# A conditional general path without SyncE and VectorE, the default order of its blocks, and two modulation loads merged into one

## The chip, the cores and the metric

One core of one Trainium2 chip runs the whole computation in one launch. The metric is the device time of that core in microseconds; the lower, the better. The engines are PE (matmuls; PEld is its weight load), DVE and ACT (vector and scalar work), POOL (GpSimd), and SP, which here only issues DMAs. Each engine has a sequencer that reads its own list of instructions in order; work between engines is ordered by semaphores. Sixteen DMA engines move the data.

## The reference

A transformer block on 2048 tokens of width 512: an adaptive layer norm, a linear attention of 32 heads with 16 columns each, and a gated feed-forward of width 1376. Cut to what matters:

```python
mod = (silu(c) @ w_mod).reshape(1, 6, 1, -1)
sa, ca, ga, sb, cb, gb = (mod[:, i] for i in range(6))
h = layernorm(x) * (1 + ca) + sa
q, k, v = split(h @ wqkv)                       # 32 heads of 16
phi(t) = concat(softmax(t @ w_phi), softmax(-(t @ w_phi)))
o = phi(q) @ (phi(k)^T v) / (phi(q) . sum_s phi(k) + 1e-6)
x = x + ga * (o @ wo)
h = layernorm(x) * (1 + cb) + sb
x = x + gb * ((sigmoid(h @ w_gate) * (h @ w_up)) @ w_down)
```

The kernel's main path takes the softmaxes' exponentials without subtracting the maximum first. That is safe while the logits are small. So the kernel works out a bound on them and writes a flag, 0 or 1. With 1, a second, general path computes everything again with the maximum subtracted and overwrites the output. With the inputs that are timed here the flag is 0 and the general path is not run.

## The kernel before, in words

**Tiling.** The tokens are 16 tiles of 128. The first part normalises each tile, transposes it into `h1T`, and builds K, V and their product over all tiles. The second takes the tiles in chunks of 1, 1, 2, 4, 4 and 4: attention output, output projection, second norm, feed-forward. A tile's result is summed by DVE from PE's `y_ps` and the residual (task `fin`, L905) and stored by SP (task `st`, L907). The last chunk's sums run in the order 12, 13, the first half of 15, 14, and then the second half of 15, which is the last store, of 64 KB.

**Order.** A planner written into the kernel (`Graph.order`) lists every piece of work as a task with an assumed cost, a due time and a release time, and simulates five engines and one DMA queue; the order that comes out is the order in which the instructions are written to each engine's list. Tables of hand-set shifts (`DUE`, `REL`, `ENG`) move single tasks. Loads are tasks on SP; a load's release time is the earliest moment in the planner's clock. The planner lets a load of a number of bytes end at a fixed rate after the one before it.

**Modulation weights.** `w_mod` has six column groups of 512. Two loads bring groups 0 and 1 early. Three more follow on SP at L965: `ga` (group 2), `m2` (groups 3 and 4), `gb` (group 5). After them comes `wo` (L966), then four transposing DMAs into `h1T` (L1111), then the feed-forward weights. Groups 3 and 4 are read by `modc2` (L1015), group 5 by `gb` (L1198), both about 58 us into the run.

**Semaphores of DMAs.** The framework gives DMAs eight semaphores in turn, each DMA the next one, and a DMA on a semaphore waits until the DMA that used it before has landed. A DMA that runs on all 16 DMA engines raises its semaphore once for each. SP issues 71 DMAs in the main path (18 loads, 36 transposes and 17 stores) and ACT issues 2.

**The conditional.** Before the sum of tile 12 the flag is read into a register of each engine that will need it (`load_flag`, L913; the loads are the `TENSOR_LOAD` at L914). After the whole main path comes

```python
    with tc.If(fv_box[0] > 0, preferred_fallthrough_block=False):   # L1306
        emit(order2)
```

`order2` is a second plan, `G2`, which holds the general path: `features` (L1241) for the softmaxes, and the same `downstream` as the main path, with its transposing DMAs and stores on SP and its vector work on DVE. All five engines take part, so each of them has a compare-and-branch at L1306. Where the flag is 0, an engine passes through an arm in which it raises semaphores by what the skipped body would have added, so that the waits that follow hold for either arm. `preferred_fallthrough_block=False` puts that arm directly behind the compare, and the body behind the arm.

**The end.** After the conditional (these instructions carry L1333) SP waits for every semaphore still in use, and then all engines pass through an exchange of semaphores and a drain, by which the kernel ends.

Of the kernel before, what the change touches and what calls it, by code (L numbers as in the profile page):

```python
# [21 lines left out]
F_LAST = F - (FT - 1) * P  # L22
NG = 8
VC = DH + 1
# [402 lines left out]
def kernel(  # L427
# [56 lines left out]
    VS = 4  # L484
# [41 lines left out]
    def bank(name, shape=None, dtype=FP32):  # L526
        return Buf("bank", shape or [P, 512], dtype, name)

    def small(name, shape):
        return Buf(name if name in CAPS else "ks", shape, FP32, name)  # L530

    def emit(order):
        for t in order:
            for b in t.bufs:
                if b.cls not in ("h2", "hm", "vaug"):
                    get(b)
            t.fn(t.eng)
# [4 lines left out]
    def kv_tasks(G, acc, t, ph, va, due, parts=((0, 8),), chain=()):  # L542
        for a, b in parts:
            def kv(e, a=a, b=b):
                for g in range(a, b):
                    pe.matmul(acc[g // 4][:, (g % 4) * HC:(g % 4 + 1) * HC], lhsT=ph[:, g * P:(g + 1) * P],  # L546
                              rhs=vaug[va.slot][:, 4 * g:4 * g + 4, :].rearrange("p h d -> p (h d)"),
                              start=(t == 0 and g % 4 == 0), stop=(t == NT - 1), skip_group_check=True)
            halves = [("kvacc", h) for h in range(2) if a < 4 * h + 4 and b > 4 * h]
            G.add(f"kv{t}.{a}", {"PE": 0.031 * (b - a)}, kv, r=[("phi", t, a), ("vaug", t)], w=[*halves, *chain],  # L550
                  bufs=[ph, va] + [acc[h] for _, h in halves], due=due)
# [359 lines left out]
    fv_box = []  # L911

    def load_flag():  # L913
        fv_box.append(nc.values_load(flag[0:1, 0:1], min_val=0, max_val=1,  # L914
                                     skip_runtime_bounds_check_because="written as 0 or 1"))

    def bound_tasks(G, due):
        for j in range(KT):
# [42 lines left out]
    load_x("x2", 8, 12, LX[0])  # L961
    load_x("x3", 12, 16, LX[1])
    load("wq", ["wq"], lambda e: sp.dma_start(wqk_sb[:, :, 0:D], wqkv_v[:, :, 0:D]), 512 * K1, LD[0], rel=LD[0])
    for nm, c0, c1, due in (("ga", 2, 3, LD[1]), ("m2", 3, 5, LD[2]), ("gb", 5, 6, LD[3])):
        load("wm" + nm, ["wmod_" + nm], lambda e, c0=c0, c1=c1: sp.dma_start(wmod_sb[:, :, c0 * D:c1 * D], wmod_v[:, :, c0 * D:c1 * D]), (c1 - c0) * 512 * K1, due, rel=due)  # L965
    load("wo", ["wo_raw"], lambda e: sp.dma_start(wo_sb[:], A_wo.rearrange("(j p) n -> p j n", p=P)), 512 * K1, LD[4], rel=LD[4])  # L966
    load("wg", ["wg"], lambda e: sp.dma_start(wg_sb[:], B_w_gate.rearrange("(j p) n -> p j n", p=P)), 1376 * K1, LD[5], rel=LD[5])
# [171 lines left out]
    for t in range(NT):  # L1139
# [8 lines left out]
        def f_v(e, t=t, vp=vp):  # L1148
            for j in range(KT):
                pe.matmul(vp[:], lhsT=h1T[:, j, t * P:(t + 1) * P], rhs=wv_sb[:, j, :], start=(j == 0), stop=(j == KT - 1))  # L1150
# [44 lines left out]
    def f_mm(e, ps, c0):  # L1195
        for j in range(KT):
            pe.matmul(ps[:], lhsT=scb[:, j, :], rhs=wmod_sb[:, j, c0:c0 + D], start=(j == 0), stop=(j == KT - 1))
    G.add("gb", {"PE": 0.87}, lambda e: f_mm(e, gb_ps, 5 * D), r=["scb", "wmod_gb"], w=["gb"], bufs=[gb_ps], due=MISC[2])  # L1198
    G.add("gbc", {"ACT": 0.6}, lambda e: act.mul(gb_bc[:], gb_ps[:], 0.5), r=["gb", "modc2ps"], w=["gbc"], bufs=[gb_ps], due=MISC[2] + 1.0)
    ga_sb = Buf("r2k", [P, D], FP32, "ga_sb")  # L1200
    G.add("ga", {"PE": 0.87}, lambda e: f_mm(e, ga_ps, 2 * D), r=["scb", "wmod_ga"], w=["ga"], bufs=[ga_ps], due=MISC[2])
# [34 lines left out]
    order = G.order()  # L1236
    emit(order)

    G2 = Graph(CAPS)

    def features(t, side, key):  # L1241
        sv = "p (h s j) -> p s h j" if side else "p (s h j) -> p s h j"

        pk = bank("pk_g")

        def f1(e):
            for j in range(KT):
                pe.matmul(pk[:], lhsT=h1T[:, j, t * P:(t + 1) * P], rhs=wqk_f[:, j, side * D:(side + 1) * D], start=(j == 0), stop=(j == KT - 1))
        G2.add(f"gp{side}{t}", {"PE": 0.9}, f1, w=[("gp", side, t), "chain"], bufs=[pk])
        ext = small("ext", [P, 2, H])  # L1250
        dd = [Buf("r2k", [P, H, DH], FP32, "dd") for _ in range(2)]
        ph = Buf("r2k", [P, 2 * H * DH], BF16, "gphi")

        def f2(e):
            pv = pk[:].rearrange("p (h j) -> p h j", j=DH)
            dve.tensor_reduce(ext[:, 0], pv, axis=AX.X, op=ALU.max)
            dve.tensor_reduce(ext[:, 1], pv, axis=AX.X, op=ALU.min)
            for s in range(2):
                dve.tensor_tensor(dd[s][:], pv, ext[:, s].unsqueeze(2).to_broadcast([P, H, DH]), op=ALU.subtract)

        def f3(e):
            for s in range(2):
                act.activation(dd[s][:], dd[s][:], ACT.Exp, scale=1.0 - 2.0 * s)

        def f4(e):
            for s in range(2):
                dve.tensor_reduce(ext[:, s], dd[s][:], axis=AX.X, op=ALU.add)
            dve.reciprocal(ext[:], ext[:])
            for s in range(2):
                dve.tensor_tensor(ph[:].rearrange(sv, s=2, j=DH)[:, s], dd[s][:],  # L1270
                                  ext[:, s].unsqueeze(2).to_broadcast([P, H, DH]), op=ALU.mult)
        G2.add(f"gd{side}{t}", {"DVE": 2.8}, f2, r=[("gp", side, t)], w=[("gd", side, t), "chain"], bufs=[pk, ext] + dd + [ph])
        G2.add(f"ge{side}{t}", {"ACT": 1.2}, f3, r=[("gd", side, t)], w=[("ge", side, t), "chain"], bufs=dd)
        G2.add(f"gn{side}{t}", {"DVE": 2.8}, f4, r=[("ge", side, t)], w=[key, "chain"], bufs=[ext] + dd + [ph])
        return ph

    acc = [bank(f"gacc{i}") for i in range(2)]
    for t in range(NT):
        ph = features(t, 1, ("phi", t, 0))
        vp = bank("gv")  # L1280
        va = Buf("vaug", None, None, "gva")

        def f_v(e, t=t, vp=vp):
            for j in range(KT):
                pe.matmul(vp[:], lhsT=h1T[:, j, t * P:(t + 1) * P], rhs=wv_sb[:, j, :], start=(j == 0), stop=(j == KT - 1))
        G2.add(f"gV{t}", {"PE": 0.9}, f_v, w=[("v", t), "chain"], bufs=[vp], due=t)
        G2.add(f"gva{t}", {"ACT": 0.6}, lambda e, vp=vp, va=va: act.copy(vaug[va.slot][:, :, 0:DH], vp[:].rearrange("p (h d) -> p h d", d=DH)),
               r=[("v", t)], w=[("vaug", t), "chain"], bufs=[vp, va], due=t)
        kv_tasks(G2, acc, t, ph, va, t, chain=["chain"])
    kvbd_tasks(G2, acc)  # L1290
    eT2 = [Buf("eT", [P, NG, 512], BF16, f"geT{cq}") for cq in range(4)]
    for cq in range(4):
        for tl in range(4):
            t = 4 * cq + tl
            ph = features(t, 0, ("gphq", t))
            tp = bank("gtp", [P, NG, P], BF16)

            def f_t(e, ph=ph, tp=tp):
                for g in range(NG):
                    pe.transpose(tp[:, g, :], ph[:, g * P:(g + 1) * P], ident[:])  # L1300
            G2.add(f"gT{t}", {"PE": 0.5}, f_t, r=[("gphq", t)], w=[("gT", t), "chain"], bufs=[ph, tp], due=100.0 + t)
            G2.add(f"gTc{t}", {"ACT": 1.0}, lambda e, cq=cq, tl=tl, tp=tp: act.copy(eT2[cq][:, :, tl * P:(tl + 1) * P], tp[:]),
                   r=[("gT", t)], w=[("eT", cq, tl)], bufs=[tp, eT2[cq]], due=100.0 + t)
    downstream(G2, eT2, 200.0, False)
    order2 = G2.order()
    with tc.If(fv_box[0] > 0, preferred_fallthrough_block=False):  # L1306
        emit(order2)


# [28 lines left out]
```

## Time and profile before

| | us |
|---|---|
| runs | 216.2, 216.68, 217.49; median 216.68 |
| span of the profiled execution | 215.3 |
| PE busy | 202.7 (94%) |
| DVE busy | 166.1 (77%) |
| ACT busy | 113.0 (53%) |
| POOL busy | 101.3 (47%) |

The span runs from the first to the last instruction of the profiled execution; the time of a run also holds what lies around it. Register, branch, semaphore and DMA-issuing instructions are not counted as busy. By stretch, on PE:

| stretch, us | PE busy, us | granted clock |
|---|---|---|
| 0 to 60 | 55.86 | 1.00 |
| 60 to 90 | 29.24 | 1.00 |
| 90 to 145 | 53.62 | 1.00 |
| 145 to 198 | 52.74 | 1.00 |
| 198 to 216 | 11.20 | 0.88 |

Instruction code is itself brought in by DMA: the profile lists two queues of the kind "instruction", q8 with 14 packets of 16 KB and q14 with 15 packets, most of 8 KB. Each such packet runs on one of the sixteen DMA engines.

### The profile page before, as it was taken

How to read it: one execution, taken by the hardware profiler on the slowest of the kernel's cores; microseconds unless marked ns; L12 is line 12 of the kernel's file. 1: busy time of each engine (PE TensorE's matmuls, PEld its weight loads, DVE VectorE, ACT ScalarE, POOL GpSimd, SP SyncE). 2: the span in 40 equal slices, each digit the busy share in tenths (PEclk: the TensorE clock that was granted, in tenths of full speed). 3: DMA queues.
4: the chain of work that ended last, by engine and by line, in shares of the span. 5: the costliest groups of instructions: out<-in, count | busy, mean ns of one | idle time of the engine just before them, and what ended most of it. 6: DMA issues, size and time to landing. Idle time of an engine off the chain costs nothing.

```text
span 215.3 us, 4319 instructions
## 1 busy us (share of the span) xinstructions
PE 202.7 (94%) x1512; PEld 113.4 (53%) x1539; DVE 166.1 (77%) x447; ACT 113.0 (53%) x278; POOL 101.3 (47%) x133
## 2 busy tenths in 40 slices
PE   7998998999999999989999999999999999999980
PEld 2744454555666577857964544454444444444450
DVE  3799999988689999859989978999899871237340
ACT  3699987998959894345442233643211651235000
POOL 3859999999969999511552222403205210000000
PEclk9999999999999999999999999999999999999996
DMA  6997997970000210250614110233201231000111
GB/s 183 371 255 167 372 193 164 411 246 0 0 3 0 52 26 5 59 90 1 99 24 72 27 28 7 68 73 74 52 14 37 52 73 50 0 0 0 55 50 34
DMA packets 31423, 18.76 MB, mean 87 GB/s; under 512 B 20673, under 2 KB 29346, under 8 KB 31394
## 3 DMA queue, kind: packets, MB, share of 16 engines
q1 hardware_dynamic: 30864, 18.39, 33.2%
q8 instruction: 14, 0.23, 0.4%
q14 instruction: 15, 0.12, 0.2%
q10 hardware_dynamic: 530, 0.02, 0.1%
HBM read 11.58 MB, written 2.10 MB: 64 GB/s over the span
## 4 chain that ended last, share of the span: by engine, by line
PE 70%; DVE 9%; DMA 8%; SPq 4%; issue 2%; ACT 2%; POOL 1%; DVEq 0%; POOLq 0%
PE y_ps L895 16%; PE u_ps L854 15%; PE g_ps L854 15%; PE a_ps L762 5%; PE v_ps L1150 4%; DMA wqk_sb<-in_A_wqkv_dram 4%; PE k_ps L1146 3%; PE q_ps L1224 3%; SPq L1044 3%; DVE u L735 2%; DMA oT<-o 2%; DMA x_sb<-in_A_x_dram 2%; PE num L645 2%; PE kvacc L546 2%; PE g_ps L856 1%
## 5 line engine op out<-in xcount | busy, mean ns | idle before, releaser
L864 ACT ACTIVATE tg<-g_ps 128x512 bf16<-128x512 f32 (+4 forms) x66 | 28.9, 453 | 57.7 <-PE g_ps L854 43.8
L875 DVE SCALAR_TENSOR_TENSOR wmod_sb<-tg,u_ps 128x512 bf16<-128x512 bf16 (+4 forms) x63 | 29.7, 494 | 17.3 <-PE u_ps L854 9.4
L895 PE MATMUL y_ps<-wd_sb,wmod_sb 128*128 128x512 bf16 (+3 forms) x178 | 41.3, 366 | 0.4
L753 POOL TENSOR_TENSOR o<-u 128x512 bf16<-128x512 f32 x14 | 17.7, 1268 | 32.0 <-DVE u L720 15.0
L1168 POOL TENSOR_TENSOR phi<-e,ks 128x1024 bf16<-128x1024 bf16 (+2 forms) x22 | 31.4, 1454 | 0.5 <-DVE ks L1178 0.3
L854 PEld LDWEIGHTS <-wg_sb 128*128 128x128 bf16 (+1 forms) x252 | 21.6, 99 | 16.2 <-issue 1.0
L854 PEld LDWEIGHTS <-wu_sb 128*128 128x128 bf16 (+1 forms) x252 | 21.8, 99 | 15.2
L895 PEld LDWEIGHTS <-wmod_sb 128*128 128x128 bf16 (+1 forms) x187 | 17.9, 98 | 16.4
L854 PE MATMUL u_ps<-wT_sb,wu_sb 128*128 128x512 bf16 (+2 forms) x123 | 23.3, 322 | 0.2
L854 PE MATMUL g_ps<-wT_sb,wg_sb 128*128 128x512 bf16 (+2 forms) x121 | 23.2, 321 | 0.1
L854 PE MATMUL g_ps<-wqk_sb,wg_sb 128*128 128x128 bf16 (+4 forms) x127 | 19.8, 287 | 0.5 <-DVE wqk_sb L828 0.4
L1165 DVE TENSOR_REDUCE ks<-e 128x64 f32<-128x1024 bf16 (+2 forms) x22 | 19.7, 906 | 0.6 <-ACT e L1162 0.6
L854 PE MATMUL u_ps<-wqk_sb,wu_sb 128*128 128x128 bf16 (+4 forms) x127 | 19.6, 287 | 0.1
L905 DVE TENSOR_TENSOR ot<-y_ps,x 128x512 bf16<-128x512 f32 (+1 forms) x17 | 11.2, 656 | 9.8 <-PE y_ps L895 9.8
L1162 ACT ACTIVATE e<-k_ps 128x512 bf16<-128x512 f32 (+2 forms) x44 | 18.3, 499 | 0.3 <-POOL phi L1168 0.3
L762 PE MATMUL a_ps<-wo_sb,oT 128*128 128x512 bf16 x62 | 16.3, 379 | 1.2 <-DMA oT<-o 1.0
L1229 ACT ACTIVATE eT<-q_ps 128x512 bf16<-128x512 f32 x32 | 16.8, 618 | 0.9 <-PE q_ps L1224 0.9
L1146 PE MATMUL k_ps<-wqk_f,h1T 128*128 128x512 bf16 x60 | 15.9, 379 | 1.1 <-ACT h1T L1126 0.8
L1150 PE MATMUL v_ps<-wv_sb,h1T 128*128 128x512 bf16 x63 | 15.8, 379 | 0.1
L1224 PE MATMUL q_ps<-h1T,wqk_f 128*128 128x512 bf16 x60 | 15.1, 378 | 0.1
L1075 DVE BATCH_NORM_STATS2 st<-x_sb 128x6 f32<-128x512 bf16 x16 | 10.8, 676 | 3.3 <-DMA x_sb<-in_A_x_dram 3.3
L767 DVE TENSOR_TENSOR x<-a_ps,x_sb 128x512 f32<-128x512 f32 x16 | 10.9, 684 | 2.5 <-PE a_ps L762 2.3
(154 smaller groups left out, 322.3 us busy)
## 6 DMA issues: line engine op xcount, KB each, us to landing
wmod_sb<-in_w_mod_dram SPq DMA_DIRECT2D x4, 512.0 KB, 6.5
out_dram<-ot SPq DMA_DIRECT2D x15, 128.0 KB, 1.7
x_sb<-in_A_x_dram SPq DMA_DIRECT2D x3, 512.0 KB, 7.5
wg_sb<-in_B_w_gate_dram SPq DMA_DIRECT2D x1, 1376.0 KB
wu_sb<-in_B_w_up_dram SPq DMA_DIRECT2D x1, 1376.0 KB, 9.4
wd_sb<-in_B_w_down_dram SPq DMA_DIRECT2D x1, 1280.0 KB, 12.2
wqk_sb<-in_A_wqkv_dram SPq DMA_DIRECT2D x2, 512.0 KB, 4.3
wmod_sb<-in_w_mod_dram SPq DMA_DIRECT2D x1, 1024.0 KB, 8.3
```

The lines of the kernel that those rows point to most:

```text
L753: G.add(f"o{t}", {"POOL": 1.3, "DVE": 0.62}, lambda e, ub=ub, o=o: engine(e).tensor_tensor(o[:], ub[0][:].rearrange("p h d -> p (h d)"), u ...
L762: pe.matmul(ap_[:], lhsT=oT[:, j, :], rhs=wo_sb[:, j, :], start=(j == 0), stop=(j == KT - 1))
L854: pe.matmul(ps[:fsz, 0:n], lhsT=w[:, j, ft * P:ft * P + fsz], rhs=h[:, j, 0:n], start=(j == 0), stop=(j == KT - 1))
L864: G.add(f"tg{k}.{ft}", {"ACT": 0.13 + n * 0.00083}, lambda e, tg=tg, g_ps=g_ps, fsz=fsz, n=n: act.activation(tg[:fsz, 0:n], g_ps[:fsz, 0:n ...
L875: dve.scalar_tensor_tensor(hm_all[:fsz, hm[k].slot, ft, 0:n], tg[:fsz, 0:n], 1.0, u_ps[:fsz, 0:n], op0=ALU.add, op1=ALU.mult)
L895: pe.matmul(y[:, 0:c1 - c0], lhsT=hm_all[:fsz, hm[k].slot, ft, tl * P:(tl + 1) * P], rhs=wd_sb[:fsz, ft, c0:c1], start=(ft == 0), stop=(ft ...
L1146: pe.matmul(kp[:], lhsT=h1T[:, j, t * P:(t + 1) * P], rhs=wqk_f[:, j, D:2 * D], start=(j == 0), stop=(j == KT - 1))
L1150: pe.matmul(vp[:], lhsT=h1T[:, j, t * P:(t + 1) * P], rhs=wv_sb[:, j, :], start=(j == 0), stop=(j == KT - 1))
L1162: act.activation(ee[:, ha:hb, s, :], kp[:, ha * DH:hb * DH].rearrange("p (h j) -> p h j", j=DH), ACT.Exp, scale=1.0 - 2.0 * s)
L1165: dve.tensor_reduce(ks[:, ha:hb].rearrange("p h s -> p (h s)"), ee[:, ha:hb].rearrange("p h s j -> p (h s) j"), axis=AX.X, op=ALU.add)
L1168: pool.tensor_tensor(ph[:, ha * 32:hb * 32].rearrange("p (h j) -> p h j", j=DH), ee[:, ha:hb].rearrange("p h s j -> p (h s) j"), ks[:, ha: ...
L1224: pe.matmul(qp[:], lhsT=wqk_f[:, j, blk * P:(blk + 1) * P], rhs=h1T[:, j, cq * 512:(cq + 1) * 512], start=(j == 0), stop=(j == KT - 1))
```

## The change

Four things. The flag is read on PE, ACT and POOL only. The loads `m2` and `gb` become one load of groups 3 to 5 (1536 KB), and the task `gb` reads from it; the main path then has 72 DMAs. The general path is no longer planned: it is written out tile by tile, with PE, ACT and POOL alone. Maxima and sums that DVE took with one reduction become chains of halvings on POOL, reciprocals become two POOL instructions, transposes go through PE and ACT, and one POOL DMA stores the whole output. And the conditional is opened without `preferred_fallthrough_block`.

```diff
     def load_flag():
-        fv_box.append(nc.values_load(flag[0:1, 0:1], min_val=0, max_val=1,
-                                     skip_runtime_bounds_check_because="written as 0 or 1"))
+        fv_box.append(nc.values_load(flag[0:1, 0:1], engines=[mybir.EngineType.PE, mybir.EngineType.Activation, mybir.EngineType.Pool],
+                                     min_val=0, max_val=1, skip_runtime_bounds_check_because="written as 0 or 1"))
...
-    for nm, c0, c1, due in (("ga", 2, 3, LD[1]), ("m2", 3, 5, LD[2]), ("gb", 5, 6, LD[3])):
+    for nm, c0, c1, due in (("ga", 2, 3, LD[1]), ("m2", 3, 6, LD[2])):
         load("wm" + nm, ["wmod_" + nm], lambda e, c0=c0, c1=c1: sp.dma_start(wmod_sb[:, :, c0 * D:c1 * D], wmod_v[:, :, c0 * D:c1 * D]), (c1 - c0) * 512 * K1, due, rel=due)
...
-    G.add("gb", {"PE": 0.87}, lambda e: f_mm(e, gb_ps, 5 * D), r=["scb", "wmod_gb"], w=["gb"], bufs=[gb_ps], due=MISC[2])
+    G.add("gb", {"PE": 0.87}, lambda e: f_mm(e, gb_ps, 5 * D), r=["scb", "wmod_m2"], w=["gb"], bufs=[gb_ps], due=MISC[2])
...
-    G2 = Graph(CAPS)
...
-    downstream(G2, eT2, 200.0, False)
-    order2 = G2.order()
-    with tc.If(fv_box[0] > 0, preferred_fallthrough_block=False):
-        emit(order2)
+    def gen_fold(src, n, op, name):
...
+        while n > 1:
+            n //= 2
+            a, b = src[:, :, 0:n], src[:, :, n:2 * n]
+            if op == ALU.add:
+                pool.tensor_tensor(t[:, :, 0:n], a, b, op=ALU.add)
...
+    def gen_features(t, side):
...
+            m = gen_fold(ps[:], DH, ALU.min if s else ALU.max, "g_ex")
+            pool.tensor_tensor(dd[:], ps[:], m.unsqueeze(2).to_broadcast([P, H, DH]), op=ALU.subtract)
+            act.activation(dd[:], dd[:], ACT.Exp, scale=1.0 - 2.0 * s)
+            gen_recip(ext[:], gen_fold(dd[:], DH, ALU.add, "g_sum"), [P, H])
+            pool.tensor_tensor(ph[:, s], dd[:], ext[:].unsqueeze(2).to_broadcast([P, H, DH]), op=ALU.mult)
...
+    with tc.If(fv_box[0] > 0):
+        gen_keys()
+        for t in range(NT):
+            gen_tokens(t)
+        pool.dma_start(o_v[:, :, :], x_sb[:])
```

More of the change, by code (lines that the diff above doesn't have):

```diff
@@ L1237 @@
     emit(order)
-    G2 = Graph(CAPS)
[L1241 to L1283, printed above, removed]
+    def gen_tile(tag, shape, dtype, name):
+        return cst.tile(shape, dtype, name=name, tag=tag, bufs=1)
+    def gen_bank(i, shape=None, dtype=FP32):
+        return psp.tile(shape or [P, 512], dtype, name=f"g_bank{i}", tag=f"bank{i}", bufs=1)
+    def gen_fold(src, n, op, name):
+        r = src.shape[1]
+        t, d = gen_tile("r2k5", [P, r, n // 2], FP32, name), None
+        if op != ALU.add:
+            d = gen_tile("r2k4", [P, r, n // 2], FP32, name + "d")
+        while n > 1:
[3 more added lines that the diff above has]
+                pool.tensor_tensor(t[:, :, 0:n], a, b, op=ALU.add)
+            else:
+                a, c = (b, a) if op == ALU.min else (a, b)
+                pool.tensor_tensor(d[:, :, 0:n], a, c, op=ALU.subtract)
+                pool.tensor_scalar(d[:, :, 0:n], d[:, :, 0:n], 0.0, None, op0=ALU.max)
+                pool.tensor_tensor(t[:, :, 0:n], b, d[:, :, 0:n], op=ALU.subtract if op == ALU.min else ALU.add)
+            src = t
+        return t[:, :, 0]
@@ new lines, in gen_recip @@
+    def gen_recip(dst, src, shape):
+        half = mhalf[:, 0:1]
+        for _ in shape[1:-1]:
+            half = half.unsqueeze(1)
+        pool.tensor_tensor(dst, src, half.to_broadcast(shape), op=ALU.pow)
+        pool.tensor_tensor(dst, dst, dst, op=ALU.mult)
+    def gen_features(t, side):
+        pk = gen_bank(0)
+        for j in range(KT):
+            pe.matmul(pk[:], lhsT=h1T[:, j, t * P:(t + 1) * P], rhs=wqk_f[:, j, side * D:(side + 1) * D], start=(j == 0), stop=(j == KT - 1))
+        ps = gen_tile("x10", [P, H, DH], FP32, "g_pk")
+        act.copy(ps[:].rearrange("p h d -> p (h d)"), pk[:])
+        ph = gen_tile("r2k0", [P, 2, H, DH], BF16, "g_phi")
+        for s in range(2):
+            dd = gen_tile(f"x1{1 + s}", [P, H, DH], FP32, "g_dd")
+            ext = gen_tile(f"ks{s}", [P, H], FP32, "g_ext")
+            m = gen_fold(ps[:], DH, ALU.min if s else ALU.max, "g_ex")
[3 more added lines that the diff above has]
+            pool.tensor_tensor(ph[:, s], dd[:], ext[:].unsqueeze(2).to_broadcast([P, H, DH]), op=ALU.mult)
+        return ph[:].rearrange("p s h d -> p (s h d)")
@@ L1284, in f_v, with gen_keys @@
+    def gen_keys():
+        acc = [gen_bank(1 + i) for i in range(3)]
+        for t in range(NT):
+            ph = gen_features(t, 1)
+            vp = gen_bank(4)
             for j in range(KT):
                 pe.matmul(vp[:], lhsT=h1T[:, j, t * P:(t + 1) * P], rhs=wv_sb[:, j, :], start=(j == 0), stop=(j == KT - 1))
-        G2.add(f"gV{t}", {"PE": 0.9}, f_v, w=[("v", t), "chain"], bufs=[vp], due=t)
-        G2.add(f"gva{t}", {"ACT": 0.6}, lambda e, vp=vp, va=va: act.copy(vaug[va.slot][:, :, 0:DH], vp[:].rearrange("p (h d) -> p h d", d=DH)),
-               r=[("v", t)], w=[("vaug", t), "chain"], bufs=[vp, va], due=t)
@@ L1289 @@
[L1289 to L1303, printed above, removed]
@@ L1304 @@
-    downstream(G2, eT2, 200.0, False)
-    order2 = G2.order()
-    with tc.If(fv_box[0] > 0, preferred_fallthrough_block=False):
-        emit(order2)
+            va = vaug[t % VS]
+            act.copy(va[:, :, 0:DH], vp[:].rearrange("p (h d) -> p h d", d=DH))
+            for g in range(NG):
+                pe.matmul(acc[g // 3][:, (g % 3) * 136:(g % 3 + 1) * 136], lhsT=ph[:, g * P:(g + 1) * P],
+                          rhs=va[:, 8 * (g % 4):8 * (g % 4) + 8, :].rearrange("p h d -> p (h d)"),
+                          start=(t == 0 and g % 3 == 0), stop=(t == NT - 1), skip_group_check=True)
@@ new lines, in gen_keys @@
+        for g in range(NG):
+            kv = gen_tile("x10", [P, 8, VC], FP32, "g_kv")
+            act.copy(kv[:].rearrange("p h c -> p (h c)"), acc[g // 3][:, (g % 3) * 136:(g % 3 + 1) * 136])
+            pool.tensor_tensor(kvbd[:, g, 0:P].rearrange("p (h d) -> p h d", d=DH), kv[:, :, 0:DH], bm, op=ALU.mult)
+            z = gen_tile("ks0", [P, 8], FP32, "g_z")
+            pool.tensor_scalar(z[:], kv[:, :, DH], 0.5e-6, None, op0=ALU.add)
+            pool.tensor_tensor(kvbd[:, g, P:P + 8], z[:], bm[:, :, 0], op=ALU.mult)
@@ L1311 @@
+    with tc.If(fv_box[0] > 0):
+        gen_keys()
+        for t in range(NT):
+            gen_tokens(t)
+        pool.dma_start(o_v[:, :, :], x_sb[:])
 _INS = ['A_x', 'A_wqkv', 'A_w_phi', 'A_wo', 'B_x', 'B_w_gate', 'B_w_up', 'B_w_down', 'c', 'w_mod']
```

67 lines of the change are left out of this document (added).

## The prediction

> **What bounds the kernel now.** I read the shares first: PE is busy 94% of the span, its clock is full until the last slice, and the chain of waits is 70% PE. Nothing in the diff touches a PE instruction of the main path, so the time can only move where PE is *not* the bound: at the load it merges, and after PE's last matmul. So I went to the end. The last pieces of the chain of waits (start us, length us, what), then the timeline from 209.2 us on:
>
> ```profile
> 203.87 5.40 PE y_ps L895 x35
> 209.27 0.02 issue
> 209.29 0.42 DVE ot L905
> ```
> ```profile
> 209.29 0.42 DVE L905 TENSOR_TENSOR ot<-y_ps,x 128x256 bf16<-128x256 f32 x1 [0.51 <-PE y_ps L895]
> 209.74 0.33 SPq L907 DMA_DIRECT2D out_dram<-ot  x1
> ```
>
> The last useful act is the issue of the last store at 209.74; the span ends at 215.3 (the last semaphore event at 215.26). So 5.5 us are tail. What fills them are sequencer instructions, which the page does not count as busy; they show when the line of the conditional (L1306) and the line of the kernel's end (L1333) are asked for. Columns: count, duration ns min/median/max, first and last start in us.
>
> ```profile
> L1306 SPq EVENT_SEMAPHORE  x8: 17/17/17, 212.8 to 213.3; - x8
> L1306 SPq COMPARE_BRANCH  x2: 43/48/53, 210.1 to 213.4; - x2
> L1306 PEldq COMPARE_BRANCH  x2: 95/1890/3686, 206.4 to 209.4; - x2
> L1306 ACTq COMPARE_BRANCH  x2: 38/44/49, 198.7 to 199.0; - x2
> L1306 POOLq COMPARE_BRANCH  x2: 38/42/45, 177.2 to 177.4; - x2
> ...
> L1333 SPq EVENT_SEMAPHORE  x10: 17/28/28, 213.9 to 215.2; - x10
> L1333 SPq DRAIN  x3: 7/7/13, 214.4 to 214.8; - x3
> ```
>
> Each engine meets two branches: a compare that falls through into the "flag is 0" arm, where semaphores are raised by what the skipped body would have added, and a jump over the body. SP, which issues all 17 stores, raises eight DMA semaphores there, and the first it asks for is that of the last store, so all eight stand behind its landing. On PE the jump alone takes 3.686 us.
>
> **The tail as a sum.** Times to the hundredth are the trace's instruction records. Landing L = 212.81. Eight raises, 212.83 to 213.41: 0.58. Jump until SP's next instruction at 213.92: 0.51. Eight final waits to 214.44: 0.52, or 0.065 each. Drains and the exchange between the five engines, to 215.26: 0.82. From L to the end: 2.45.
>
> And L itself is late. The first line below are landings (min/median/max) of the three stores issued between 205.2 and 208.8; the other lines are the DMA view of 211.2 to 212.3:
>
> ```profile
> DMA to landing us min/median/max: 1.5/1.7/1.7
> ```
> ```profile
> DMA  0000000000000000000010100101101001010000
> q1 hardware_dynamic: 9, 0.00, 3.3%
> ```
>
> The last store takes 3.07, not 1.7. Its data left at 210.6 to 210.9 on 15 of 16 DMA engines, whose marks were all in by 211.45 (1.70 after issue). Eight packets, one engine's share, left only from 211.77 on. At 210.73 a single 16 KB instruction packet (queue q8) began, and it lasted 1.05. The pace of q8, one packet for some 250 PE instructions, says that this queue is PE's; the packet comes 1.28 after PE's jump at 209.45. So PE's jump is paid for by the store: 1.36 us.
>
> **The change, part by part.**
>
> 1. *SP and DVE leave the conditional.* Their flag loads and branches go, and SP's eight raises. Of the 2.45 behind L that removes 0.58 + 0.51 = 1.09.
>
> 2. *The last store on the last semaphore.* DMAs take eight semaphores in turn. There are 71 on SP and 2 on ACT, 73 in all, so the last one sits on the first semaphore; with 72 it sits on the eighth. SP's final waits go in that order, so seven are done between 210.1 and 210.7, under the store. Removed: 7 x 0.065 = 0.46. Left behind L: 0.02 + 0.065 + 0.82 = 0.90. The general path's single store goes out on POOL and may add one more final wait: 0.065 if it comes after the eighth, else nothing; I take nothing.
>
> 3. *Default block order.* I read it as body first: the compare itself is the jump, and the flag-0 arm stands behind the body and runs into the end. PE's sequencer runs ahead of its array; it reached the compare at 206.39, with matmuls queued until 209.25. A jump there, at the 3.69 of the row, is over at 210.08, PE drains at about 210.3, and nothing waits. Its packet would run from 206.39 + 1.28 = 207.67 to 208.7. In that stretch no store has data moving: the one issued at 206.16 has landed by 207.7, the next leaves from 209.6. So the last store gets the usual 1.70: L = 209.74 + 1.70 = 211.44, which is 1.36 off. ACT and POOL also jump at the compare. At PE's price they are back by 202.4 and 181; their last work ends at 198.9 and 177.2, and the exchange is after 211, so that is hidden by 9 us or more.
>
> 4. *Flag loads of DVE and SP*:
>
> ```profile
> L914 DVEq TENSOR_LOAD <-flag x1: 542/542/542, 200.2 to 200.2; - x1
> L914 SPq TENSOR_LOAD <-flag x1: 513/513/513, 201.3 to 201.3; - x1
> ```
> DVE's next sum starts at 202.12 when PE's y is done, and SP's next store at 202.84 when DVE is: both loads lie under PE. Nothing gained; uncovered they would be 0.54 and 0.51.
>
> 5. *Merged load.* SP saves one issue (0.51) at 20.1 and then waits for POOL until 25.77 as before. The bytes and the place in the queue are the same. The modulation column now comes with the gb piece, so columns that landed at 27.8 land at about 29.2; the matmuls reading them run at 58.4, 29 us later. The rows become 3 KB for 2 + 1 KB; at the packets' median of 84 ns for 2 KB and 46 for 1 KB, 32 of each for a DMA engine take 4.2, and one 3 KB packet between 109 (the row of 2.75 KB) and 130 gives 3.5 to 4.2. So everything behind it is 0 to 0.7 earlier. Behind it are wo (needed after 50) and the transposes into h1T (3.1/4.1/5.9 to landing). ACT waits 1.8 once for these, but the chain of waits runs through K and V matmuls there. I take 0, and -0.7 to +0.4 for the range: the loss is a transpose meeting an instruction packet, whose long ones took 1.5 to 1.9 at 28.9 and 31.0 and are off the chain today. Every later DMA waits for the semaphore's user eight before it. Only one such wait shows in SP's list (0.6, on wp_sb), ahead of the merge; behind it the users are the same or earlier ones.
>
> 6. *Order of the main path.* The planner sees one task fewer. The gb load's only reader is released at 58.2 or later, and the merged load ends in the planner's queue when the gb load did (it is issued while the one before is still moving, at one rate per byte), so wo and all that follows have the same times there: same order. The general path is planned apart, and no instruction of it is in the trace.
>
> **Sum.** -1.09 - 0.46 - 1.36 + 0 = -2.91: the profiled execution's 215.3 becomes 212.4. Outside the span lie 216.68 - 215.3 = 1.4 to the median of the runs, which I keep: **213.8**.
>
> The Trainium skill, "DMA: Bandwidth & Descriptors", section "Anatomy of one DMA", puts most of a fixed 2.0 us on the write receipt, plus bytes over 436 GB/s; that is fitted on the GpSimd path, and the rows above (1.5 to 1.7) are shorter. By it the last store would land no sooner than 2.15 after issue, an estimate, and the time would be 214.3.
>
> **The rivals.**
>
> - *The landing gains nothing, -1.55: 215.1.* After PE's jump a second 16 KB packet followed, 0.91 behind the jump's end (214.04 after 213.13). Moved forward it falls at 210.08 + 0.91 = 210.99, and the last store's data ended at 210.92. 0.1 us earlier and it hits as today. The same result comes if the runs around the median were not hit before: 216.2 to 217.49 is as wide as the hit. For: the margin is 0.07. Against: the estimate does fall behind the data.
> - *PE's jump takes the place of SP's waits, -1.25: 215.4.* If the default order still has PE raise its semaphore first and jump afterwards, PE drains at 213.26 as today, the exchange takes 0.75 after it, the end is 214.0. It decides once SP is ready before 213.2, as it then is. For: nothing in the trace shows the other order. Against: "fall through into the skipped arm" was asked for by name and is now not asked for.
> - *The change doesn't do what it says, -0.5: 216.2.* SP stays in the conditional because the final waits want all arms equal; only the semaphore's place is gained.
> - *Slower: the planner's order moves after all, 217.9.* Before 60 us PE is idle 60.0 - 55.9 = 4.1 (stretch table); were the order redrawn so that this idle time doubled, +4.1 - 2.9 = +1.2. It decides from 4.0 us lost. Against it: point 6, and that only loads lie between 18 and 25 on SP.
>
> **Chances.** Forecast 0.42, no gain in landing 0.28, PE's jump 0.12, not done 0.09, order 0.09. What a measurement can tell from no change is about 0.5%, 1.1 us; 215.1 and 215.4 lie 0.5 and 0.2 beyond it, so a little of them goes to "same": faster 0.75, same 0.14, slower 0.11. The forecast's own range is 213.1 to 214.5 (point 5's bounds). The range to hold 8 in 10 reaches over the next three cases, 213.1 to 216.2.
>
> **What would show it.** Right: no L1306 line on SP or DVE; PE's one compare near 206.4 lasting some 3.7; the q8 packet near 207.7 and none between 210.5 and 211; SP's last waits ending 0.1 after a landing 1.7 behind the issue; the last matmul still at 209.25. Wrong: a landing of 3 us again (first rival), PE's drain past 213 (second), SP raising semaphores (third), the last matmul later than 209.7 (fourth).

## The result, and the profile after

| | before | after |
|---|---|---|
| runs, median (lowest to highest), us | 217.02 (216.20 to 218.04), 6 runs | 214.06 (212.93 to 216.08), 6 runs |
| ratio, 95% interval | | 0.9875 (0.9838 to 0.9913) |
| profiled execution: span, us | 215.3 | 213.3 |
| last `y_ps` matmul begins, us | 208.98 | 208.20 |
| last store issued; landed | 209.74; 212.81 | 208.97; 212.32 |
| landing to the span's end | 2.45 | 0.93 |

The predicted 213.8 is within 0.3 of the median. No run lies near that median, though: three of the six took 212.93 to 213.33 and three 214.80 to 216.08. The steps behind the forecast do not all fit either. Of the 2.0 between the two profiled executions (215.26 to 213.25) the part behind the landing gave 1.52, as predicted. The landing itself, where 1.36 was expected, came 0.29 *later* behind its issue (3.35 after 3.07). And 0.78 came from work that the change was not thought to touch.

In the trace after, the conditional carries L1380 and the kernel's end L1410. The first fence is the conditional's line, the second the end's line on SP (count, duration ns min/median/max, first and last start in us):

```profile
L1380 POOLq COMPARE_BRANCH  x1: 45/45/45, 176.4 to 176.4; - x1
...
L1380 ACTq COMPARE_BRANCH  x1: 50/50/50, 197.9 to 197.9; - x1
L1380 ACTq EVENT_SEMAPHORE  x1: 17/17/17, 200.4 to 200.4; - x1
L1380 PEldq COMPARE_BRANCH  x1: 3631/3631/3631, 205.6 to 205.6; - x1
```
```profile
L1410 SPq EVENT_SEMAPHORE  x10: 17/28/28, 209.3 to 213.2; - x10
L1410 SPq DRAIN  x3: 7/7/13, 212.4 to 212.7; - x3
```

SP and DVE are gone from the conditional. Each of the other engines has one compare where it had two, and on PE that compare is the jump: 3.63 long, from 205.62, while its array works until 208.5. SP's final waits begin at 209.3, and by the instruction records seven of the eight are over at 209.74, under the store. Only the eighth, at 212.34, stands behind the landing, and the first drain follows at 212.40.

The last two stores' time to landing (min/median/max us), and the bandwidth from 208 to 214 us in 40 slices of 0.15 us:

```profile
DMA to landing us min/median/max: 1.7/2.5/3.4
```
```profile
GB/s 0 0 0 0 0 55 328 355 137 0 0 3 218 294 3 0 0 0 0 0 0 3 10 10 3 0 0 0 0 0 0 0 0 0 0 0 0 0 55 0
```

The last store's data leave at 209.8 to 210.1 (218 and 294 GB/s; the second slice also holds a 16 KB code packet of queue q8, begun at 210.01). Then, a microsecond later, 3, 10, 10 and 3 GB/s: one engine's eight packets, held back until the code packet, which took 1.25, was through. Fifteen of the store's sixteen marks came in by 210.50, the last at 212.32. This is the picture of before, but with another packet: not the first behind PE's jump (206.65, harmless, as forecast), but the second.

The 0.78 is in the chain of waits between 88 and 95 us (start us, length us, what). First before, then after:

```profile
88.76 4.16 DMA oT<-o
92.92 0.05 issue
92.97 1.04 PE a_ps L762 x4
```
```profile
90.15 3.84 DMA wqk_sb<-xn
93.99 0.02 issue
94.02 0.02 ACT wqk_sb L832
```

Up to 91 us both traces run alike within 0.35. Then each has a transposing DMA that lands 1.4 to 1.8 later than the usual 2.4, but not the same one: before it is `oT<-o`, for which PE's output projection waits; after, it is the next one, `wqk_sb<-xn`, which a feed-forward chunk needs later. By the matmuls' records the work after, 0.13 behind until 91 us, is 0.78 ahead from 97 us to the end. The planned order of each engine is the same in both.

### The profile page after: what moved, and what is told of

The parts are those of the page before. It is cut to its first block, busy times and chain, and to the rows that moved or that the text cites. A ratio compares the mean times of both kernels' runs of the same rounds, so it can differ in the third digit from the quotient of the medians.

```text
span 213.3 us, 4297 instructions
## 1 busy us (share of the span) xinstructions
PE 202.6 (95%) x1512; PEld 112.6 (53%) x1539; DVE 166.1 (78%) x447; ACT 112.9 (53%) x278; POOL 101.3 (48%) x133
## 4 chain that ended last, share of the span: by engine, by line
PE 67%; DVE 12%; DMA 8%; SPq 5%; issue 3%; ACT 2%; POOL 2%; DVEq 0%; POOLq 0%
PE y_ps L895 16%; PE g_ps L854 15%; PE u_ps L854 15%; PE a_ps L762 5%; DMA wqk_sb<-in_A_wqkv_dram 4%; PE q_ps L1224 3%; PE v_ps L1150 3%; SPq L1044 3%; PE k_ps L1146 2%; DVE u L735 2%; DMA x_sb<-in_A_x_dram 2%; PE num L645 2%; DMA wqk_sb<-xn 2%; PE kvacc L546 1%; PE g_ps L856 1%
## 5 line engine op out<-in xcount | busy, mean ns | idle before, releaser
L864 ACT ACTIVATE tg<-g_ps 128x512 bf16<-128x512 f32 (+4 forms) x66 | 28.9, 453 | 56.5 <-PE g_ps L854 42.4
L1213 POOL TENSOR_TENSOR wd_sb<-wd_sb,wmod_sb 128x512 bf16<-128x512 bf16 x11 | 12.5, 1168 | 0.0
```

Source lines behind the costliest of these rows:

```text
L864: G.add(f"tg{k}.{ft}", {"ACT": 0.13 + n * 0.00083}, lambda e, tg=tg, g_ps=g_ps, fsz=fsz, n=n: act.activation(tg[:fsz, 0:n], g_ps[:fsz, 0:n ...
```

## The experiments

Two theories follow from the profile. **A code packet that meets a DMA's data delays that DMA by more than a microsecond**, at the end (the store) and near 91 us (the transposes), and the timing of a few tenths decides what it meets. Against it: the landing and the work's pace depend on the block order, on the merged load, or on the missing flag reads themselves. Ten runs were made in three sets; the kernel before ran beside each set (medians 216.28, 216.58 and 216.69).

**The change again.** No edit.

> The changed kernel itself, for more runs on the chip of the other three. Theory: in the profile of the change, PE's second packet of code (16 KB) began at 210.01, inside the 209.80 to 210.15 in which the last store's data moved, and one DMA engine's mark came 1.8 us after the other fifteen. The margin is near nothing, so runs should fall in two groups, spans near 211.4 (missed) and near 213.2 (hit), and the median time anywhere from 212.9 to 215. Rival: the packet has nothing to do with it and the spans scatter about one value, 213.3, by 0.5.

Median 214.71 (213.63 to 215.06), ratio 0.9905 (0.9870 to 0.9939). Spans 212.8 to 213.3 in five runs, 211.8 in one; in the first set of the changed kernel there were three at 211.2 to 211.5. The profiled run again has the late mark: landing 3.38. So the changed kernel's time is two-valued, and the upper value is the more common (8 of 12 runs above 212.5). That the lower one is the store that was missed is an inference from the spans; no execution of that group was profiled for this kernel.

**The arm first.** The old block order in the changed kernel:

```diff
-    with tc.If(fv_box[0] > 0):
+    with tc.If(fv_box[0] > 0, preferred_fallthrough_block=False):
```

> The changed kernel with the flag-0 arm put directly behind the compare again, so that PE jumps after its last matmul. Theory: PE's compare falls through near 205.6, a jump of 3.7 starts 0.2 after the last matmul's end, PE drains 4.0 after that end and the exchange (0.75) follows: 4.7 to 4.8 from the last matmul's end to the end of the span in every run, against 4.8 (hit) or 2.9 (missed) for the change; its fastest runs some 1.8 slower than those of the changed kernel, span not below 213.0. Rival: the order of the arms does not matter, since SP is what the end waits for; then the fastest spans stay at 211.4.

Median 214.92 (214.20 to 215.26), ratio 0.9914 (0.9881 to 0.9947). In the trace of this run, PE at the conditional and at the kernel's end:

```profile
L1380 PEldq COMPARE_BRANCH  x2: 95/1740/3386, 206.0 to 209.0; - x2
```
```profile
L1410 PEldq DRAIN  x2: 8/40/73, 212.5 to 212.9; - x2
```

PE's jump begins at 209.0 again. The store lands at 212.09 (2.77 behind its issue) and SP is ready at 212.24, but the exchange cannot begin before PE's drain at 212.47. From the end of the last matmul to the end of the span it takes 4.50. The expectation had 4.7 to 4.8, with a jump of 3.7 where 3.39 was measured, and no span below 213.0; three of the six are 212.5 to 212.9. The fastest is 1.3 and 0.7 above the fastest of the two sets of the change, where 1.8 was expected. So with this order PE's own jump is a second wait of nearly the same length as the hit store: in this profile even a missed store would have gained nothing. That is why the order matters, and why its median is so close to that of the change with the store hit (0.2 between them): what the default order is worth is seen only in runs where the store is missed.

**Three modulation loads.** The changed kernel with the old loads, 73 DMAs:

```diff
-    for nm, c0, c1, due in (("ga", 2, 3, LD[1]), ("m2", 3, 6, LD[2])):
+    for nm, c0, c1, due in (("ga", 2, 3, LD[1]), ("m2", 3, 5, LD[2]), ("gb", 5, 6, LD[3])):
```

> The changed kernel with the three modulation loads of before (73 DMAs, the last store on the first of eight semaphores again). Theory: seven of SP's final waits come behind the landing again, 1.35 to 1.4 from landing to the end for 0.93 now: +0.45 in every run. The main path up to the last matmul is not changed by the loads as such; it may differ by 0 to 0.8 either way by which DMA PE's code packets meet. Rival: the merged load gives the main path its 0.8 (last matmul's end 209.25 before, 208.48 after), so here it ends at 209.2 again and the loss is 1.2.

Median 215.54 (213.49 to 216.77), ratio 0.9944 (0.9918 to 0.9971). SP's end in the trace of this run:

```profile
L1410 SPq EVENT_SEMAPHORE  x10: 17/28/28, 213.4 to 214.7; - x10
```

The first final wait, at 213.4 where the change has 209.3, is now the one for the last store (landed 213.35). The seven others queue behind it until 213.86, and the end is 1.45 behind the landing instead of 0.93: 0.52 for the place among the semaphores. The rest of the difference in this profile (its work ends 1.07 later; at 91 us it was 0.04 behind, from 95 us on 1.07) is the packet near 91, which here met `oT<-o`.

**Three more matmuls.** The changed kernel, with PE's compare pushed back by three small matmuls whose results nobody reads:

```diff
+    pad = psp.tile([P, 512], FP32, name="pad", tag="bank7", bufs=1)
+    for i in range(3):
+        pe.matmul(pad[:, i:i + 1], lhsT=ident[:], rhs=ident[:, 0:1], start=True, stop=True)
```

> The changed kernel with three more matmuls of one column on PE ahead of the conditional, whose results nobody reads. They delay PE's compare by six places in its list, about 0.65 us. Theory: the jump's packet runs from about 207.3 to 208.5, before the data of the store ahead of the last (208.9), and the second packet begins at 210.6 to 210.7, after the last store's data (to 210.15). So the last store lands 1.5 to 1.6 after its issue in every run, PE drains near 210.1 which is still before that landing, and the span is 211.4 in one group: about 1.8 off the hit runs of the changed kernel, median time 212.9 to 213.2. Rival: the packet is not the cause, and the runs look like those of the changed kernel.

Median 213.17 (212.74 to 213.75), ratio 0.9848 (0.9816 to 0.9879): faster than the change, though it does more work. The landing of the last store, which is alone in the window here, and the bandwidth as above:

```profile
DMA to landing us min/median/max: 1.5/1.5/1.5
```
```profile
GB/s 0 0 239 362 260 14 0 0 123 277 38 0 109 0 0 0 0 0 0 0 0 0 55 0 0 0 0 0 0 0 0 0 0 0 0 0 0 0 0 0
```

The store's data (123, 277, 38) are through before the code packet (109 GB/s in one slice is its 16 KB), nothing is left over, and all sixteen marks are in 1.53 behind the issue. All that the prediction's point 3 asked for is here: the jump early, the packets off the store, the landing undisturbed.

**Twenty-three.** The same edit with `range(23)`, so that it is the first packet that falls on the store.

> The changed kernel with 23 one-column matmuls on PE ahead of the conditional (their results are not read), where the run with three put PE's second code packet behind the last store's data. Theory (a code packet that meets the last store's data is the whole of the landing's delay): the compare comes some 2.6 us later than with none, near 208.3, its jump is over near 211.8, and now the FIRST packet, some 1.1 behind the compare (209.4 to 210.6), lies on the store's data: landing 3.1 to 3.4 behind the issue again, end 0.9 after it, 4.8 after the last y matmul; every run in the upper group, median 214.7 to 215.2. Rival (three matmuls helped because something else at the end was moved, the more the better): 213.2 or less, landing 1.5 to 1.7.

Median 215.00 (214.38 to 215.89), ratio 0.9928 (0.9905 to 0.9952), all eight runs in the upper group. Compare at 208.20, first packet 209.35, 0.65 behind the store's issue; landing 3.09. The store's landing and SP's final waits:

```profile
DMA to landing us min/median/max: 3.1/3.1/3.1
```
```profile
L1414 SPq EVENT_SEMAPHORE  x10: 17/28/2786, 209.1 to 213.1; - x10
```

So three matmuls do not help by being there; they help by where they put the packet. It is the landing that shows this, and not the time. The jump took 3.91 here and was over at 212.11, and one of SP's final waits (the one of 2.786, from 209.47) ended only when PE raised its semaphore at 212.17, which is behind the landing at 211.79. The end came 1.41 behind the landing, where 0.9 was expected, and with a missed store it would have come no sooner.

**The merged load alone**, in the kernel before (the change's second and third piece of the diff and nothing else).

> The kernel before with the merged modulation load alone: 72 DMAs, the last store on the eighth semaphore; conditional untouched. Theory: of SP's eight raises seven are done before the landing, so landing to the span's end falls from 2.45 by 7 x 0.083 = 0.58 x 7/8 = 0.51 to 1.94; the eight final waits stay behind the jump. Nothing before the conditional changes but by where code packets fall: 0.5 faster, ratio 0.9975. Rival (the merged load itself is what made the changed kernel's work end 0.8 sooner): last matmul near 208.2 instead of 209.0, 1.3 faster, ratio 0.994.

Median 215.83 (215.27 to 216.59), ratio 0.9949 (0.9927 to 0.9971), 0.75 faster by the medians and 1.1 by the ratio: between the two expectations. The conditional's and the end's line on SP:

```profile
L1306 SPq EVENT_SEMAPHORE  x8: 17/17/17, 209.4 to 212.2; - x8
```
```profile
L1333 SPq EVENT_SEMAPHORE  x10: 17/28/28, 212.8 to 214.0; - x10
```

Seven raises are done from 209.4 on; the eighth waits for the landing at 212.15, and from there to the end it takes 1.94 instead of 2.45, as expected. But the profiled run's last matmul is at 208.14, 0.84 earlier than before, as the rival had it. Its code packet near 91 missed `oT<-o`. By this run alone the merged load could be the cause; the next experiment and the one with the code moved decide that it is not.

**The default order alone**, in the kernel before.

```diff
-    with tc.If(fv_box[0] > 0, preferred_fallthrough_block=False):
+    with tc.If(fv_box[0] > 0):
```

> The kernel before with the default block order alone; all five engines still in the conditional. Theory: the compare is the jump on every engine; PE's comes near 206.4 while matmuls are queued, SP's is over before the landing, so 0.51 goes from behind the landing (2.45 to 1.94: raises 0.58, waits 0.52, exchange 0.82 stay), and PE's second packet falls 0.8 behind its jump's end, which meets the last store's data in most runs: landing 3.0 to 3.4 with the hit (median 0.3 to 0.6 faster, ratio 0.998), 1.5 to 1.7 without (2 us faster in those runs). Rival (point 3 as predicted, no hit): every run some 1.9 faster, ratio 0.991.

Median 215.97 (214.22 to 216.88), ratio 0.9963 (0.9937 to 0.9989). Three of twelve runs have spans of 212.5 to 212.9, the others 213.8 to 215.1: the two groups that the theory asks for. The profiled run is of the lower one. The compares on DVE, SP and PE are single, SP's at 209.1 is over before the landing, and 1.95 is left behind the landing (expected 1.94). Its store was not missed cleanly: landing 2.23. PE's second packet came 1.24 behind the issue, but it was not alone. An 8 KB code packet of queue q14 had begun 0.77 behind the issue, at 209.48, and lasted 0.34; it came 1.21 behind DVE's compare at 208.27, and so is probably DVE's. Both are in the bandwidth from 209.3 to 211.3 us (40 slices of 0.05 us), as 164 and 338 GB/s:

```profile
GB/s 0 0 0 164 10 154 246 297 256 174 103 31 338 10 10 10 0 0 0 0 0 0 164 0 0 0 0 0 0 0 0 0 0 0 0 0 0 0 0 0
```

By the packets' records four of the store's packets left only 1.20 to 1.38 behind the issue, when all the others were out, and took 68 to 101 ns each for the usual 27. This kernel has three loads and all flag reads, and yet its packet near 91 missed `oT<-o` and its last matmul is at 207.95. So the 0.78 belongs neither to the merged load nor to the missing reads.

**The code moved by eight instructions.** The changed kernel with four one-column matmuls among the warming ones in the first 4 us (their results are not read); with their weight loads, all later PE code lies eight instructions further on.

```diff
+            for i in range(4 if nm == "warm0" else 0):
+                pe.matmul(ps[:, i:i + 1], lhsT=wd_sb[:, FT - 1, 0:P], rhs=wd_sb[:, FT - 1, 0:1], start=True, stop=True)
```

> The changed kernel with four more one-column matmuls on PE among the warming ones at the start (their results are not read), so that every later PE instruction lies four places, eight with the weight loads, further on in the code, and each code packet is asked for that much earlier in the work: the one near 91.1 some 0.5 us earlier, 90.6. Theory (the changed kernel's work ended 0.8 sooner because that packet missed the transposing DMA oT<-o and met the next one): it meets oT again, whose landing goes from 2.4 to 4.1 behind its issue, and the last matmul comes 0.6 to 0.9 later; the median rises to 215.2 to 215.6. Rival (the merged load or the missing flag reads gave it): no change, 214.4 to 214.7, last matmul where it was.

Median 215.63 (213.66 to 216.90), ratio 0.9943 (0.9912 to 0.9974): above both medians of the change. Its chain of waits near 90 us:

```profile
88.27 4.38 DMA oT<-o
92.65 0.05 issue
92.70 1.04 PE a_ps L762 x4
```

The packet came at 90.17, met `oT<-o`, and that DMA is on the chain again as in the kernel before, with its last matmul 0.5 and 1.0 behind those in the two profiles of the change (208.71 against 208.20 and 207.76). Nothing else was edited. The interval of the ratio overlaps with those of the change, so the medians alone would not show it; the chain does.

**The three matmuls again**, unchanged.

> The changed kernel with three one-column matmuls on PE ahead of the conditional (their results are not read), run again. Theory (they set PE's jump later against the last store, whose data then pass between the two code packets): all runs in one group about 1.5 below the changed kernel's upper group, median 3.0 to 3.4 below the kernel before, landing 1.5 to 1.7 behind the issue, second packet over 1.3 behind the issue. Rival (luck of one set of runs): a part of the runs 1.5 higher, as with the changed kernel.

Median 213.12 (212.69 to 213.49), ratio 0.9845 (0.9816 to 0.9874). That is 3.57 below the kernel before beside it, a little more than the 3.0 to 3.4 expected. Twelve runs of this kernel now lie in one group, spans 210.9 to 212.0.

**Half a packet.** The same kernel, with the six warming matmuls of 512 columns at the start replaced by seventy of 44 (results not read): PE code lies 128 instructions further on.

> The same, and at the start the six warming matmuls of 512 columns are replaced by seventy of 44 (as many columns, their results are not read), so that all later PE code lies 128 instructions, half a packet, further on. The packet that lay on the transposing DMAs at 90.2 to 92.3 in every run so far is then asked for some 4 us earlier, 86.3 to 87.5, where no data move between two groups of transposes (86.0 to 88.2 in the trace of the run with three matmuls). Theory (these delays are packets that meet DMAs, and any of them can be moved off): both oT<-o and wqk_sb<-xn land 2.4 behind their issue; the wait of some 1.4 for wqk_sb<-xn goes and the last matmul comes up to 1 sooner, less whatever the other packets, moved by half their distance, now meet. Rival (the delay near 91 has another cause, such as the transposes themselves): it stays, 3.8 behind the issue.

Median 213.95 (213.48 to 214.63), ratio 0.9877 (0.9847 to 0.9906): slower than without the shift. The profiled run, 0.7 above that median, is the slowest of the six. The transposes `oT<-o` of 86 to 97 us (time to landing), and the chain of waits at 78 us:

```profile
DMA to landing us min/median/max: 2.4/2.4/2.4
```
```profile
78.08 4.50 DMA oT<-o
```

The packet now lies at 88.54, off the transposes, and the delay near 91 is gone: between 80 and 95 us this kernel makes up 0.53 on its unshifted twin. It had lost 2.55 by then, though. 1.5 of that came with a packet at 80.03 that met an earlier `oT<-o` (an 8 KB code packet, 1.45 long from 80.68, followed it; their shares were not told apart), the rest arose in the first 43 us. A delay can be moved off one DMA, and lands on another.

**All profiles together.** Times are from the trace's records, behind the issue of the DMA named; the first table is sorted by where the packet near 91 us lies, the second by where the one at the end lies.

| kernel | packet behind issue of `oT<-o` | `oT<-o` lands | next `wqk_sb<-xn` lands |
|---|---|---|---|
| half a packet | -2.10 | 2.40 | 2.48 |
| code moved by eight | 1.90 | **4.38** | 3.48 |
| three loads | 1.91 | **4.28** | 3.42 |
| before | 2.11 | **4.16** | 3.39 |
| after; default order alone | 2.22; 2.22 | 2.42; 2.42 | 3.84; 4.09 |
| twenty-three; change again | 2.23; 2.25 | 2.41; 2.40 | 3.91; 3.91 |
| merged alone; arm first | 2.33; 2.35 | 2.40; 2.41 | 3.98; 4.05 |
| three matmuls, again and first | 2.39; 2.66 | 2.41; 2.41 | 4.10; 3.86 |

| kernel | packet behind issue of the last store | store lands |
|---|---|---|
| twenty-three; arm first | 0.65; 0.72 | **3.09**; **2.77** |
| change again; three loads | 0.77; 0.77 | **3.38**; **3.32** |
| merged alone; before | 0.81; 0.99 | **3.25**; **3.07** |
| code moved; after | 1.00; 1.04 | **3.45**; **3.35** |
| default order alone | 1.24 | **2.23** |
| three matmuls, first and again; half a packet | 1.42; 1.50; 1.63 | 1.53; 1.53; 1.54 |

Twelve profiles of ten kernels, and in either table the place of the packet divides the late landings from the others, but for the row of the default order alone, where an 8 KB code packet was in play as well. The border for `oT<-o` is between 2.11 and 2.22. That for the store is between 1.04 and 1.24: in five profiles PE's first packet began 1.24 to 1.27 behind the issue of the first half of tile 15, also 64 KB, which landed in 1.52 to 1.53. The profile before stood 0.1 on the wrong side of the first.

The length of the packet counts as well. In the eight profiles in which a 16 KB packet met the last store's data, that packet took 1.01 to 1.55, and the store landed 1.02 to 1.05 behind the packet's end in all of them; the three late `oT<-o` landed 1.17 to 1.18 behind it. That is what a share of the data held back until the packet is through looks like, and neither the block order, the merged load nor the flag reads give it.

The Trainium skill, "Runtime: NRT & Kernel Launch", section "Instruction fetch mechanics", describes the refill in blocks of 16 KiB and a taken branch whose target has to be fetched by DMA first; both agree with the packets and jumps here (PE's jumps took 3.3 to 3.9). It calls the cost of crossing a block mostly hidden. That holds for PE itself (before, two packets fall between 145 and 198 us, and PE is busy 52.74 of these 53); the tables show that the DMA beside it pays 1.2 to 2.0.

## Why the prediction was right, and where it was not, point by point

- **Point 1** (SP and DVE leave the conditional, -1.09) and **point 2** (last store on the last semaphore, -0.46) held: 0.90 was to be left behind the landing, 0.93 was. With the three loads, thus without point 2, 1.45 is left of the 2.45: 1.00 for point 1, and 0.52 for the place. Of point 1 the parts were also seen alone in the kernel before: seven of the eight raises by the merged load (2.45 to 1.94), and SP's jump by the default order (0.50), which takes it off the path as leaving the conditional does. No run took SP and DVE out of the conditional and did nothing else. POOL's store of the general path added no final wait.
- **Point 3** was right in its mechanism and wrong in its size. Default order is body first, the compare is the jump, it runs under PE's queue (205.62 to 209.25), and the first packet hits nothing. But the 1.36 of the landing did not come in the profiled runs of the change: the second packet took the first one's place, as the first rival had it. The prediction put it 0.91 behind the jump's end, from one measurement, thus 1.25 behind the store's issue, with a margin of 0.07. In the profile after it came 1.04 behind the issue: 0.15 of the 0.21 are the distance from the jump's end (0.76), 0.06 the jump (3.63 for 3.69). In the others with this order the distance is 0.76 to 0.82, and the jumps vary from 3.33 to 3.77 where they are not preceded by 23 matmuls. A margin of 0.07 on such terms decided nothing; the rival should have had the better half of the chance. With the packet moved off, the term is there, and larger: landing 1.53. The 1.70 of the sum is what the 128 KB stores take, and the last store's fifteenth mark; the store of 64 KB in the same view, issued at 206.16, took 1.53.
- **Points 4 and 6** held: the flag reads' absence moved nothing that could be seen (the default order alone keeps them all, and its last matmul is at 207.95), and the order of the main path is unchanged.
- **Point 5** took 0 for everything ahead of PE's end. The merged load is worth nothing that could be seen, but the term was -0.78 in the profiled pair. It was not the load: the profile before happened to hold a code packet on a transpose that the chain of waits goes through. The prediction had seen such packets only at 28.9 and 31.0 and called them off the chain; the 4.16 of `oT<-o` on the chain at 88.76 was in the profile and was not read.
- **Around the span** the prediction kept 1.4. Each run's own time less its span is 1.7 to 1.9; 1.4 came from setting one span against the median of other runs.

So the mechanisms of points 1 to 3 were right, and the closeness of the number was luck. In the profiled pair the landing came out 1.65 above the forecast (1.36 not gained and 0.29 lost), and the transposes gave 0.78 that nobody had asked for; that leaves the span 0.9 above the predicted 212.4, and the profiled run took 214.99. The median came to 214.06 because three of its six runs are of the lower group and three of the upper: it lies in the gap between them, from 213.63 to 214.53, in which the changed kernel had no run in either set. Pooled over both sets, twelve runs, the median is 214.7, which is 0.4 from the first rival's 215.1 and 0.9 from the forecast's 213.8. The rival with PE's jump is refuted by PE's drain at 209.46, the one in which SP stays by the missing lines, the slower one by the unchanged order.

The best version found is the change with three idle matmuls in front of the conditional: 213.1 to 213.2, ratio 0.985. What it gains on the change alone, some 1.5, is where a code packet falls.

## What to carry to other kernels

In a kernel near its bound, the instruction queues are part of the DMA traffic: when a DMA on the chain lands late with one of its sixteen marks behind the rest (the transposes `wqk_sb<-xn` here had all of them late), look for a 16 KB code packet at its data, and for what sets the packet's time. Put no landing into a sum on a margin smaller than the spread of the terms that make it; give both values and expect a time with two values. A branch belongs where its engine has queued work, and its follow-up packets belong in the account as well.

## What the runs showed that was not expected

- A code packet of 0.9 to 1.6 on one DMA engine delays a DMA by 1.2 to 2.0 (store 1.53 to between 2.77 and 3.45, `oT<-o` 2.4 to between 4.16 and 4.38), as that engine's share of the data waits, and the DMA is not done before its slowest share. For `wqk_sb<-xn` this is not the whole account: there all sixteen marks come late (after: 3.59 to 3.84 behind the issue), and why is open.
- PE's taken jump brings a second packet 0.76 to 0.82 behind its end (0.91 in the profile before); that packet alone cost the changed kernel some 1.8 in the landing (3.35 against 1.53).
- The other engines pay for a jump taken at the compare too: ACT 2.5 (197.92 to 200.44), POOL 2.6 (176.42 to 179.0), and, with the default order alone, DVE 3.1 (208.27 to 211.4), which drained at 211.47. There it lay 0.6 ahead of SP's first drain; had SP left the conditional and the store landed 1.53 behind its issue, at 210.24, DVE's jump would have been the next wait. So it may matter that both leave together; it was not tried with DVE alone left in.
- Eight instructions at the start of a program, doing nothing, moved a DMA 85 us later onto or off the chain of waits (`oT<-o` 2.40 or 4.38 to landing).
